# Laying the score matmuls right behind the weighted sums, in one step of a software pipeline

## The chip, the core and the metric

The kernel runs on one core of a Trainium2 chip. Time is device microseconds of one launch. The core has five engines that run side by side and meet in semaphores: PE (matmuls; the trace lists its weight loads apart as PEld), ACT, DVE, POOL and SP, which here only issues DMAs. Each engine takes its instructions strictly in the order in which the program lists them.

## What is computed

Attention with heads mixed before and after the softmax, then a layer of eight experts of which each token takes one, then a dense layer. The change lies in the attention:

```python
scores = scale * np.matmul(q, k.transpose(0, 1, 3, 2))      # batch 4, 12 heads, 448 x 448, head size 64
scores = np.einsum('bhij,hg->bgij', scores, w_pre)
attn = np.exp(scores - np.max(scores, axis=-1, keepdims=True))
attn = attn / (np.sum(attn, axis=-1, keepdims=True) + 1e-09)
attn = np.einsum('bhij,hg->bgij', attn, w_post)
x = np.matmul(attn, v)                                      # to [1792, 768]
x = _moe_ref(x, ...)                                        # top 1 of 8 experts, 768 -> 1024 -> 768
return _moe2_ref(x, ...)                                    # (h - tanh h) @ w_out, 768 -> 2048 -> 768
```

The weights of the last layer arrive as words of 64 bits; the kernel converts them on DVE and POOL while the attention runs ("conversion", 96 chunks, 72 of them inside the attention).

## The kernel before

**Tiles and steps.** The queries of each batch are cut into four tiles T of 120, 120, 120 and 88 rows, 16 tiles in all. A tile's scores (12 heads, in pairs p) are written to the buffer `s_sb`, of which there are two. A DMA, the relay `sr`, regroups them into blocks of ten queries by twelve heads, 120 partitions by 448 keys; a tile has 12 blocks or, where it is short, 9. There are 180 blocks, and the loop `for s in range(NBK + LAG + 6)` handles one a step:

- PE: P(s), the head mix before the softmax (L373); DVE: its row maximum `mx` (L377); ACT: the exponential p(s) with its sum (L380).
- DVE: `emit_W(s-1)`, which folds 1/sum into the mixing weights w (L387 to L390).
- PE: T(s-2), which turns and mixes in one go (four matmuls in the source, eight in the trace, L412); ACT: its copy into A (L417).

**Side work.** A table `side`, filled ahead of the loop by `at`, `at_s` and `at_e` from the position functions `posS2` and `posAV`, says in which step the rest stands: S2(T, p), the scores of two pairs for tile T, which the blocks need some ten steps later (L330; copies to `s_sb` at L337 and L334 on ACT, L335 on DVE); AV(T, p), weighted sums of the finished tile (L430, copy xT at L432 on ACT); `tr_q` and `tr_k`, the turned operands ptq and ptk; X, the turned outputs, with routing sums; R0 to R3 and M0 to M3, routing matmuls for the experts; and `conv_do`, one chunk of the conversion: three DVE operations (L117 to L119), three POOL operations, one store.

**A turned operand** passes four engines' queues: PE turns it into PSUM, ACT copies its high part (qh L310, kh L293), DVE writes the low part (ql L311, kl L294), and DVE does the latter in the next step, ahead of that step's row maximum:

```python
            for fn, a in turns:
                flush("e")
                late2.append(("e", fn(*a)()))     # turn, high part on ACT; low part put off
            if on:
                emit_TE(i)                        # ACT: A(s-2), behind that high part
```

**PSUM** has eight banks: P takes two in turn ("b"); T, R and M share two in turn ("c"); AV has one ("d"); ptq, ptk and X share one ("e"); S2 takes two of its own for its first pair of heads, and "d" and "e" for the second. So a turned operand can't start before the one ahead of it has left "e", and S2's second pair can't start before AV's result has left "d".

**Order within a step before:** P; row maximum; W; the first of S2 and AV that the step holds; the exponential; conversion; T; turned operands; A; what is left. S2 and AV stand as a rule in different steps. The 72 conversions stand in steps that hold S2 or AV, some of them two.

Of the kernel before, what the change touches and what calls it, by code (L numbers as in the profile page):

```python
# [30 lines left out]
def body(ctx: ExitStack, tc, q, k, v, w_pre, w_post, emb, tau, w1, w2, win, wout, out):  # L31
# [8 lines left out]
    NP = H // 2  # L40
# [89 lines left out]
    if True:  # L130
# [253 lines left out]
        def emit_W(i):  # L384
            n = 12 * blocks[i][2]
            p, mx = pj[i]
            dve.tensor_scalar_add(mx[:n, 2:3], mx[:n, 1:2], 1e-9)  # L387
            dve.reciprocal(mx[:n, 3:4], mx[:n, 2:3])
            w = a2.tile([120, 120], F32, tag="w", name=f"w{i}", bufs=3)
            dve.tensor_scalar_mul(w[:n, :], wpost[:n, :], mx[:n, 3:4])  # L390
            wj[i] = w
# [250 lines left out]
    with mctx:  # L642
# [334 lines left out]
        def posS(T, p):  # L977
            f, nb = (first[T - 1], ntile[T - 1]) if T else (-12, 12)
            return f - (5 if T > 1 else 3) + (p + 0.5) * nb / 6

        def posS2(T, p):
            return posS(T, p - p % 2 + 0.5)

        def posAV(T, p):
            f, nb = first[T + 1], ntile[T + 1]
            return f + LAG + 1 + p * nb / 6
# [48 lines left out]
        CA = CONV_A  # L1035
        kinds = lambda k: [x[0] for x in side.get(k, [])]
        routed = [k for k in side if emit_R in kinds(k)]
        free = [k for k in range(12, NBK - 11) if k not in routed]
        long_ = [k for k in free if emit_AV2 in kinds(k)]
        mid = [k for k in free if emit_S2 in kinds(k) and emit_AV2 not in kinds(k)]  # L1040
        alone = [k for k in long_ if not {emit_X, tr_q, tr_k} & set(kinds(k))]
        more = CA - len(long_) - len(mid)
        steps = sorted(long_ + mid + [alone[i * len(alone) // more] for i in range(more)])
        for j, st in enumerate(steps):
            ld = max(st - 4, steps[j - 4] + 1 if j >= 4 else 0)
            assert ld < st
# [22 lines left out]
        def relay_to(i):  # L1069
            while nxt[0] <= min(i, NBK - 1) and blocks[nxt[0]][0] in sdone:  # L1070
                emit_relay(nxt[0])
                nxt[0] += 1
# [4 lines left out]
        def flush(tag=None):  # L1077
            keep = []
            while late:
                x = late.pop(0)  # L1080
                if tag in (None, x[0]):
                    y = x[1]()
                    if x[0] == "e" and callable(y):
                        late2.append((x[0], y))
                else:
                    keep.append(x)
            late.extend(keep)
            if tag:
                flush2(tag)
# [9 lines left out]
        def run_fill(fn, a):  # L1099
            tag = "d" if fn is emit_AV2 else "e"  # L1100
            if fn is emit_S2:
                flush("d")
                flush("e")
            elif fn is not emit_S:
                flush(tag)
            e = fn(*a)
            if fn in (emit_S, emit_S2):
                e()
                if a[1] + (fn is emit_S2) == NP - 1:
                    sdone.add(a[0])  # L1110
            else:
                late.append((tag, e))
# [36 lines left out]
        for s in range(NBK + LAG + 6):  # L1149
            todo = side.get(s, [])  # L1150
            fill = [x for x in todo if x[0] in PEF]
            for fn, a in todo:
                if fn in (load_q, load_k, load_v, conv_load, zero_fill):
                    fn(*a)
            flush()
            relay_to(s + NSR - 1)
            ex = emit_P(s) if s < NBK else lambda: None
            if 0 <= s - 1 < NBK:
                emit_W(s - 1)
            for fn, a in todo:  # L1160
                if fn is emit_R and a[1] in (0, 1, 3):
                    fn(*a)
            i = s - LAG
            on = 0 <= i < NBK
            fill.sort(key=lambda x: x[0] not in (emit_S, emit_S2, emit_AV2))
            if fill and fill[0][0] in (emit_S, emit_S2, emit_AV2):
                run_fill(*fill.pop(0))
            ex()
            for fn, a in todo:
                if fn is conv_do:  # L1170
                    fn(*a)
            if on:
                emit_T(i)
                T_mm(i, 0, NJ)
                flush("d")
            turns = [x for x in fill if x[0] in (tr_q, tr_k)] if on else []
            for fn, a in turns:
                flush("e")
                late2.append(("e", fn(*a)()))
            if on:  # L1180
                emit_TE(i)
            for x in fill:
                if x not in turns:
                    run_fill(*x)
            for fn, a in todo:
                if fn in (to_experts, first_gather) or fn is emit_R and a[1] in (2, 4, 5, 6):
                    fn(*a)
            for fn, a in todo:
                if fn is do1:
                    fn(*a)  # L1190
# [55 lines left out]
        for n, e in enumerate(items):  # L1246
# [39 lines left out]
            todo = []  # L1286
            if not last:
                nw1, nx = [], xtile(f"i{n + 1}")
                todo = [lambda c=c: do1(n + 1, c, nw1) for c in range(KD)]
                todo += [lambda j=j, t=t, hf=hf: xsplit(nx, t, j, hf, f"i{n + 1}") for j, t in enumerate(nxg) for hf in range(2)]  # L1290
            for ci, col in enumerate(cols):
                y = mq[0].tile([128, DM], F32, tag="y", name=f"y{nm}_{ci}", bufs=2)
                for nh in range(2):
# [13 lines left out]
                    todo = todo[k_:]  # L1307
# [324 lines left out]
```

## Time and profile before

| what | value |
| --- | --- |
| median of 3 runs | 1296.83 us (1296.11 to 1299.66) |
| the profiled execution | 1295.99 us, of which 1294.1 us are the span from first to last instruction |
| PE busy | 1283.5 us (99%) |
| DVE, ACT, POOL busy | 1003.8, 747.7, 489.4 us (78, 58, 38%) |
| chain that ended last | PE 94%, DVE 2%, DMA 2%, ACT 1% |
| granted TensorE clock | 1.000 of full speed |

The times of the prediction are made against the profiled execution, 0.84 us below the median. The end of a matmul is modelled in the trace, so the sum of PE's busy time hides short waits; starts are what to read. A step is the time from one P to the next.

### The profile page before, as it was taken

The numbers are of one execution on the slowest core, as the hardware profiler recorded it, in microseconds if no ns is written. First come the engines' busy times: TensorE is split into PE (matmuls) and PEld (weight loads), VectorE is DVE, ScalarE is ACT, GpSimd is POOL, SyncE is SP. The second block draws the span as 40 slices with busy tenths as digits, with TensorE's granted clock in tenths as the row PEclk, the third lists the DMA queues.
The fourth block names the chain that finished last, engine by engine and source line by source line (L and its number), as shares of the span: only waits on it lengthen the run. The fifth ranks groups of instructions, "written<-read, shape, count | busy, mean of one in ns | idle before, by whom it ended". The sixth has DMA issues, their size and how long they took to land.

```text
span 1294.1 us, 24851 instructions
## 1 busy us (share of the span) xinstructions
PE 1283.5 (99%) x9072; PEld 1125.4 (87%) x9072; DVE 1003.8 (78%) x2168; ACT 747.7 (58%) x1513; POOL 489.4 (38%) x497
## 2 busy tenths in 40 slices
PE   9999999999999999999999999999999999999998
PEld 6777777777777778999999999999999999999997
DVE  5877877787878677788787676788888887888886
ACT  6767666666766665555544545765444556444432
POOL 1334423351344126333223222454644544444431
PEclk9999999999999999999999999999999999999999
DMA  7887665666557458778988876321211123111102
GB/s 172 268 267 214 199 204 152 200 202 192 160 168 223 147 157 301 262 264 250 268 245 259 265 241 210 105 86 49 86 58 65 49 99 122 50 50 49 50 25 88
DMA packets 153077, 210.95 MB, mean 163 GB/s; under 512 B 57686, under 2 KB 113158, under 8 KB 152950
## 3 DMA queue, kind: packets, MB, share of 16 engines
q1 hardware_dynamic: 149680, 195.37, 49.1%
q0 software_dynamic: 2480, 12.19, 2.7%
q8 instruction: 74, 1.21, 0.4%
q10 hardware_dynamic: 790, 1.74, 0.4%
q14 instruction: 53, 0.43, 0.1%
HBM read 135.71 MB, written 35.01 MB: 132 GB/s over the span
## 4 chain that ended last, share of the span: by engine, by line
PE 94%; DVE 2%; DMA 2%; ACT 1%; issue 0%; POOL 0%; SPq 0%; DVEq 0%; POOLq 0%
PE T L412 12%; PE P L373 10%; PE AV L430 6%; PE o L1454 6%; PE o L1452 6%; PE o L1453 6%; PE h L1418 6%; PE h L1417 6%; PE h L1416 6%; PE S L330 5%; PE ypi L706 3%; PE ypi L707 3%; PE ypi L705 3%; PE hi L729 3%; PE hi L730 3%; PE hi L731 3%
## 5 line engine op out<-in xcount | busy, mean ns | idle before, releaser
L412 PEld LDWEIGHTS T<-w,p 120*112 120x112 f32 (+1 forms) x1440 | 166.1, 177 | 59.5 <-issue 46.0
L122 POOL TENSOR_TENSOR cm<-cm,ct 128x256 f32<-128x256 f32 x96 | 70.7, 736 | 313.5 <-DVE ct L119 291.6
L412 PE MATMUL T<-w,p 120*112 120x120 f32 (+1 forms) x1440 | 185.0, 272 | 0.2 <-ACT p L380 0.2
L1399 POOL TENSOR_TENSOR gl<-th,gh 128x512 fp32r<-128x512 f32 (+1 forms) x64 | 77.5, 1211 | 241.1 <-ACT gh L1398 180.4
L373 PE MATMUL P<-sr,wpre 120*120 120x448 f32 x360 | 166.3, 544 | 1.0 <-DMA sr<-ssb 1.0
L380 ACT ACTIVATE p<-P,mx 120x448 f32<-120x448 f32 x180 | 114.1, 634 | 89.9 <-DVE mx L387 76.2
L1420 ACT ACTIVATE u<-h 128x512 f32<-128x512 f32 (+1 forms) x64 | 35.0, 547 | 204.1 <-PE h L1418 204.1
L1452 PE MATMUL o<-woh,gh 128*128 128x384 f32 x448 | 151.4, 338 | 0.0
L1454 PE MATMUL o<-woh,gl 128*128 128x384 f32 x448 | 150.4, 336 | 0.0
L1453 PE MATMUL o<-wol,gh 128*128 128x384 f32 x448 | 150.1, 335 | 0.0
L1458 DVE TENSOR_TENSOR acc<-acc,o 128x384 f32<-128x384 f32 x196 | 106.5, 548 | 47.2 <-PE o L1454 47.2
L377 DVE TENSOR_REDUCE mx<-P 120x1 f32<-120x448 f32 x180 | 111.6, 620 | 28.9 <-PE P L373 26.7
L120 POOL TENSOR_TENSOR cm<-craw 128x256 f32<-128x256 f32 x96 | 66.9, 697 | 112.8 <-DMA craw<-in_moe_w_in 59.2
L417 ACT COPY A<-T 112x480 f32<-112x480 f32 x180 | 102.3, 568 | 9.7 <-PE T L412 9.7
L729 PE MATMUL hi<-xhi,w1h 128*128 128x256 f32 x336 | 95.3, 283 | 0.0
L730 PE MATMUL hi<-xli,w1h 128*128 128x256 f32 x336 | 95.2, 283 | 0.0
L731 PE MATMUL hi<-xhi,w1l 128*128 128x256 f32 x336 | 95.2, 283 | 0.0
L705 PE MATMUL ypi<-w2hi,hhi 128*128 128x384 f32 x272 | 93.9, 345 | 0.0
L430 PEld LDWEIGHTS AV<-A,v 112*64 112x64 f32 x1536 | 73.9, 137 | 21.8 <-issue 10.7
L706 PE MATMUL ypi<-w2li,hhi 128*128 128x384 f32 x272 | 91.2, 335 | 0.2 <-DVE w2li L673 0.2
L707 PE MATMUL ypi<-w2hi,hli 128*128 128x384 f32 x272 | 91.2, 335 | 0.0
L121 POOL TENSOR_SCALAR cm<-cm 128x256 f32<-128x256 f32 x96 | 85.9, 895 | 8.4
(299 smaller groups left out, 3436.3 us busy)
## 6 DMA issues: line engine op xcount, KB each, us to landing
sr<-ssb SPq DMA_DIRECT2D x176, 210.0 KB
r<-in_moe_w SPq DMA_DIRECT2D x72, 384.0 KB
r<-in_moe_w SPq DMA_DIRECT2D x52, 512.0 KB
craw<-in_moe_w_in SPq DMA_DIRECT2D x48, 256.0 KB
craw<-in_moe_w_out SPq DMA_DIRECT2D x48, 256.0 KB
wor<-wo_d SPq DMA_DIRECT2D x16, 768.0 KB
raw<-wi_d SPq DMA_DIRECT2D x15, 768.0 KB
wi_d<-cm SPq DMA_DIRECT2D x48, 128.0 KB
```

What stands on the lines that cost most here:

```text
L373: pe.matmul(pt[:n, :S], wpre[:n, :n], t[:n, :], start=True, stop=True)
L412: pe.matmul(pt[:CP, c * n:(c + 1) * n] if m == 10 else pv[:, c], p[:n, c * CP:(c + 1) * CP], w[:n, :] if m == 10 else wv, start=True, stop ...
L430: pe.matmul(pt[64 * hh:64 * hh + 64, x * 120:x * 120 + n], vt[b, p + x][:, hh, c, :], A[T][:, c, 2 * (p + x) + hh, :n], start=c == 0, stop ...
L705: pe.matmul(pt[:, :384], a, wh[:, n0:n0 + 384], start=f == 0, stop=False)
L706: pe.matmul(pt[:, :384], a, wl[:, n0:n0 + 384], start=False, stop=False)
L707: pe.matmul(pt[:, :384], l, wh[:, n0:n0 + 384], start=False, stop=f == KF - 1)
L729: pe.matmul(pt[:, :256], wh[:, sl], xh[:, c, :], start=c == 0, stop=False)
L730: pe.matmul(pt[:, :256], wh[:, sl], xl[:, c, :], start=False, stop=False)
L731: pe.matmul(pt[:, :256], wl[:, sl], xh[:, c, :], start=False, stop=c == KD - 1)
L1452: pe.matmul(pt[:, :384], gh[:, sl], wo[0][:, f, n0:n0 + 384], start=f == 0, stop=False)
L1453: pe.matmul(pt[:, :384], gh[:, sl], wo[1][:, f, n0:n0 + 384], start=False, stop=False)
L1454: pe.matmul(pt[:, :384], gl[:, sl], wo[0][:, f, n0:n0 + 384], start=False, stop=f == GF - 1)
```

## The change

Three things. `posS2` puts S2(T, p) into the steps of AV, two places on: pairs 0 and 2 into the steps of AV(T-3, 2) and AV(T-3, 4), pair 4 into that of AV(T-2, 0). Since `tr_q`, `load_q`, `tr_k` and `load_k` are placed relative to `posS2`, they move with it. In a step with both, AV now comes ahead of S2, and the exponential and the conversion stand between them; T follows S2. And the conversions are dealt out anew: one a step over the steps with S2, AV or X, with a second one only where chunks are left.

```diff
         def posS2(T, p):
-            return posS(T, p - p % 2 + 0.5)
+            p -= p % 2
+            if p == NP - 2 and T > 1:
+                return posAV(T - 2, 0)
+            return posAV(T - 3, p + 2) if T > 2 else posS(T, p + 0.5)
...
-        alone = [k for k in long_ if not {emit_X, tr_q, tr_k} & set(kinds(k))]
-        more = CA - len(long_) - len(mid)
-        steps = sorted(long_ + mid + [alone[i * len(alone) // more] for i in range(more)])
+        both = [k for k in long_ if emit_S2 in kinds(k)]
+        rest_ = [k for k in free if emit_X in kinds(k) and k not in long_ + mid]
+        room = sorted(long_ + mid + rest_)
+        more = max(0, CA - len(room))
+        room = sorted(room + [both[i * len(both) // more] for i in range(more)])
+        steps = [room[i * len(room) // CA] for i in range(CA)]
...
             fill.sort(key=lambda x: x[0] not in (emit_S, emit_S2, emit_AV2))
+            fill.sort(key=lambda x: x[0] is not emit_AV2)
+            if len(fill) > 1 and fill[0][0] is emit_AV2 and fill[1][0] is emit_S2:
+                run_fill(*fill.pop(0))
+                ex()
+                ex = lambda: None
+                for fn, a in todo:
+                    if fn is conv_do:
+                        fn(*a)
+                todo = [x for x in todo if x[0] is not conv_do]
             if fill and fill[0][0] in (emit_S, emit_S2, emit_AV2):
                 run_fill(*fill.pop(0))
             ex()
```

In the rows of the built program below, the first number in a name is the step of P, T, w and p (P19 is step 19) or the tile of the rest, the last one only tells buffers apart.

PE from step 19 before: AV and S2 in two steps, each followed by its T.

```order
L373 MATMUL P19_932<-sr19_692,wpre_133 120x448
L430 MATMUL AV0_2_941<-A0_434,v0_2_443 64x120 x8
L430 MATMUL AV0_2_941<-A0_434,v0_3_463 64x120 x8
L412 MATMUL T17_968<-w17_919,p17_868 112x120 x4
L303 MATMUL ptq3_0_974<-ident_68,natq3_778 128x88 x3
L373 MATMUL P20_985<-sr20_713,wpre_133 120x448
L412 MATMUL T18_996<-w18_939,p18_916 112x120 x4
L373 MATMUL P21_1012<-sr21_759,wpre_133 120x448
L330 MATMUL S3_0_1022<-kh0_0_189,qh3_0_978 88x448 x2
L330 MATMUL S3_0_1022<-kl0_0_190,qh3_0_978 88x448 x2
L330 MATMUL S3_0_1022<-kh0_0_189,ql3_0_979 88x448 x2
```

PE in step 19 of the change, from the second half of AV: S2 follows AV, and T17 follows S2.

```order
L430 MATMUL AV0_2_942<-A0_434,v0_3_463 64x120 x8
L330 MATMUL S3_0_971<-kh0_0_189,qh3_0_899 88x448 x2
L330 MATMUL S3_0_971<-kl0_0_190,qh3_0_899 88x448 x2
L330 MATMUL S3_0_971<-kh0_0_189,ql3_0_900 88x448 x2
L330 MATMUL S3_1_0_978<-kh0_1_221,qh3_0_899 88x448
L330 MATMUL S3_1_1_979<-kh0_1_221,qh3_0_899 88x448
L330 MATMUL S3_1_0_978<-kl0_1_222,qh3_0_899 88x448
L330 MATMUL S3_1_1_979<-kl0_1_222,qh3_0_899 88x448
L330 MATMUL S3_1_0_978<-kh0_1_221,ql3_0_900 88x448
L330 MATMUL S3_1_1_979<-kh0_1_221,ql3_0_900 88x448
L412 MATMUL T17_989<-w17_914,p17_884 112x120 x4
L373 MATMUL P20_998<-sr20_713,wpre_133 120x448
```

So one T, with the whole array, that stood between AV and S2 is gone from there. Forty steps of the change read like this (15, 19, 23, ... to 162).

PE some steps on, before: a turned operand shares its step with AV, or has a step with AV or S2 on one side at least.

```order
L412 MATMUL T20_1069<-w20_1019,p20_990 112x120 x4
L287 MATMUL ptk1_0_1074<-ident_68,natk1_0_856 128x112 x4
L373 MATMUL P23_1087<-sr23_838,wpre_133 120x448
L430 MATMUL AV0_4_1097<-A0_434,v0_4_491 64x120 x8
L430 MATMUL AV0_4_1097<-A0_434,v0_5_516 64x120 x8
L412 MATMUL T21_1124<-w21_1066,p21_1016 112x120 x4
L303 MATMUL ptq3_1_1130<-ident_68,natq3_778 128x88 x3
L373 MATMUL P24_1141<-sr24_908,wpre_133 120x448
L412 MATMUL T22_1152<-w22_1095,p22_1063 112x120 x4
L287 MATMUL ptk1_1_1157<-ident_68,natk1_1_859 128x112 x4
L373 MATMUL P25_1176<-sr25_910,wpre_133 120x448
```

The same place of the change, steps 20 to 22: three turned operands in three steps one after the other, with nothing between them but P and T.

```order
L412 MATMUL T18_1008<-w18_940,p18_911 112x120 x4
L287 MATMUL ptk1_0_1013<-ident_68,natk1_0_778 128x112 x4
L373 MATMUL P21_1024<-sr21_759,wpre_133 120x448
L412 MATMUL T19_1035<-w19_1005,p19_937 112x120 x4
L303 MATMUL ptq3_1_1040<-ident_68,natq3_711 128x88 x3
L373 MATMUL P22_1053<-sr22_786,wpre_133 120x448
L412 MATMUL T20_1064<-w20_1032,p20_1002 112x120 x4
L287 MATMUL ptk1_1_1069<-ident_68,natk1_1_781 128x112 x4
L373 MATMUL P23_1088<-sr23_860,wpre_133 120x448
```

Such threes stand in steps 20 to 22, 24 to 26, 28 to 30, 65 to 67, 69 to 71, 73 to 75, 110 to 112, 114 to 116 and 118 to 120 (in 26, 71 and 116 the third is an X).

ACT around the routing of tile 4, before. On PE, R0 stands in step 64, ahead of AV and T62.

```order
L380 ACTIVATE p62_2603,mx62_2601<-P62_2599,mx62_2601 120x448
L417 COPY A5_2509<-T60_2636 112x48x10
L380 ACTIVATE p63_2650,mx63_2648<-P63_2646,mx63_2648 120x448
L417 COPY A5_2509<-T61_2656 112x48x10
L380 ACTIVATE p64_2668,mx64_2666<-P64_2664,mx64_2666 120x448
L432 COPY xT4_2540<-AV4_2_2682 128x240
```

ACT at the same place of the change. On PE, R0 now stands in step 63, a step without AV, straight ahead of T61; the seven DVE operations that feed it stand in step 61.

```order
L380 ACTIVATE p61_2583,mx61_2581<-P61_2579,mx61_2581 120x448
L417 COPY A5_2498<-T59_2598 112x48x10
L380 ACTIVATE p62_2610,mx62_2608<-P62_2606,mx62_2608 120x448
L310 CAST qh7_0_2625<-ptq7_0_2621 128x3x88
L417 COPY A5_2498<-T60_2616 112x48x10
L380 ACTIVATE p63_2636,mx63_2634<-P63_2631,mx63_2634 120x448
L417 COPY A5_2498<-T61_2651 112x48x10
```

What moved: the copy of T60 into A now stands behind the high part of ptq7_0, in the step just ahead of R0. M0 likewise moved from step 68, with AV, to step 67, without; R1, M1, R2 and M2 (steps 108, 112, 153, 157) read the same way.

## Rows read from the trace of the kernel before

**Rows 1.** Busy time of each engine in two stretches; x is the count of instructions.
```profile
core 0: us, PE busy (x) PEld busy (x) DVE busy (x) ACT busy (x) POOL busy (x), PEclk, DMA share, GB/s
40.00:493.00 453.00, 453.00 (x3971) 338.99 (x3969) 348.53 (x1076) 307.83 (x735) 162.16 (x223) 1.00 0.65 199
```

**Rows 2.** Timeline of steps 60 to 63, PE alone: start, length, engine, line, operation.
```profile
173.12 0.92 PE L373 MATMUL P<-sr,wpre 120*120 120x448 f32 x2
...
175.76 1.07 PE L412 MATMUL T<-w,p 120*112 120x120 f32 x8
...
176.67 0.92 PE L373 MATMUL P<-sr,wpre 120*120 120x448 f32 x2
...
177.42 0.98 PE L412 MATMUL T<-w,p 120*112 120x120 f32 x8
...
178.24 0.92 PE L373 MATMUL P<-sr,wpre 120*120 120x448 f32 x2
...
179.09 0.46 PE L330 MATMUL S<-kh,qh 64*120 64x448 f32 x2
...
179.80 0.37 PE L330 MATMUL S<-kh,qh 64*120 64x448 f32 x2
...
180.21 0.36 PE L330 MATMUL S<-kh,ql 64*120 64x448 f32 x2
...
181.41 0.92 PE L373 MATMUL P<-sr,wpre 120*120 120x448 f32 x2
```

**Rows 3.** Same timeline, ACT in step 60; in brackets idle time and releaser.
```profile
173.59 0.47 ACT L468 COPY raw<-X 88x384 f32<-88x384 f32 x1
...
174.10 0.84 ACT L477 ACTIVATE xsq<-raw 88x768 bf16<-88x768 f32 x1
...
175.87 0.36 ACT L432 COPY xT<-AV 128x240 f32<-128x240 f32 x1 [0.23 <-PE AV L430]
```

**Rows 4.** Timeline of steps 33 to 35, the chain through two turned operands.
```profile
99.58 0.92 PE L373 MATMUL P<-sr,wpre 120*120 120x448 f32 x2
...
100.54 0.62 DVE L377 TENSOR_REDUCE mx<-P 120x1 f32<-120x448 f32 x1
...
101.46 0.66 DVE L390 TENSOR_SCALAR w<-wpost,mx 120x120 f32<-120x120 f32 x1
101.47 0.92 PE L373 MATMUL P<-sr,wpre 120*120 120x448 f32 x2
...
101.89 0.45 ACT L310 CAST qh<-ptq 128x360 fp32r<-128x360 f32 x1
...
102.22 0.58 ACT L417 COPY A<-T 112x480 f32<-112x480 f32 x1
...
102.37 0.53 DVE L311 TENSOR_TENSOR ql<-ptq,qh 128x360 fp32r<-128x360 f32 x1 [0.24 <-ACT qh L310]
102.82 0.62 DVE L377 TENSOR_REDUCE mx<-P 120x1 f32<-120x448 f32 x1
...
103.73 0.28 DVE L390 TENSOR_SCALAR w<-wpost,mx 120x120 f32<-120x120 f32 x1
...
104.15 0.52 ACT L293 CAST kh<-ptk 128x448 fp32r<-128x448 f32 x1
...
104.71 0.62 DVE L294 TENSOR_TENSOR kl<-ptk,kh 128x448 fp32r<-128x448 f32 x1 [0.70 <-ACT kh L293]
...
105.25 0.62 DVE L377 TENSOR_REDUCE mx<-P 120x1 f32<-120x448 f32 x1
...
105.39 0.18 PEld L330 LDWEIGHTS S<-kh,qh 64*120 64x120 f32 x1 [0.31 <-DVE kl L294]
```

**Rows 5.** Timeline of step 62, the first and the last of seven routing operations.
```profile
180.31 0.18 DVE L498 TENSOR_TENSOR lk<-lg 128x32 f32<-128x32 f32 x1
...
181.65 0.19 DVE L508 TENSOR_TENSOR oht<-ohk,tokf 128x32 f16<-128x32 f16 x1
```

**Rows 6.** Timeline of step 178: a weight load for T and what released it.
```profile
491.70 0.89 PEld L412 LDWEIGHTS T<-w,p 120*112 120x112 f32 x8 [0.70 <-DVE idr L549]
```

## The prediction

> **What bounds the kernel now.** I read the windows first. From 40 to 493 us, the attention's steps 10 to 178, PE is busy in all 453 us, DVE in 349, ACT in 308, POOL in 162 [rows 1]. PE sets the time here, and any other engine matters only where it makes PE wait. Since matmul ends are modelled, I then read starts in PE's timeline [rows 2]. A step with only P and T takes 178.24 - 176.67 = 1.57 us, one with S2 3.17, one with AV 3.55. P to T is 0.75, T's eight matmuls take 0.82, or 0.1025 each. The other steps of the stretch repeat these lengths; a turned query adds 0.32 (101.47 - 99.58 = 1.89 [rows 4]), and I put a turned key, four transposes for three, at 1.97. So the kernel before has hardly a wait on PE, and the sum has two sides: PE work that goes, and waits that come.
>
> **What the change removes.** S2 adds 1.60 to a step. Its six pairs of matmuls go at (180.21 - 179.80) / 2 = 0.205, so 1.23 is streaming and 0.37 is the way in and out. AV adds 1.98; its 32 matmuls run two abreast, 16 places at T's 0.1025, so 1.64 is streaming and 0.34 the way in and out [rows 2]. Four switches between full and split array thus cost 0.71, one 0.18. AV, S2, T in one step has three switches where two steps had four: 0.18 saved, in 40 steps, **-7.2**. The trace has no AV with S2 straight behind it. The bounds are a passage that costs nothing (0.36 saved each, -14.4 in all) and one that costs two switches (nothing saved); I take one switch, since all four that can be read cost about the same.
> The Trainium skill bears on this one price: TensorEngine Tiling (Array Packing), section Key Properties, says that a change of tiling mode, not merely of the tile, drains the engine. AV splits the array by columns and S2 by rows, so by that rule the passage is a drain too and the sum stays; if only leaving the full array counted, the sum would be 7.2 lower. That the switches cost time [rows 2] agrees with it; no row shows this passage.
> Some waits of the kernel before go too. In steps 35, 80 and 125 S2's second pair waited for a key's low part in bank "e" (a weight load idle for 0.31, released by kl [rows 4]), 0.28 a step; T just ahead of them was 0.1 to 0.2 late behind a w that took 0.66 beside POOL in place of 0.28 [rows 4]; six S2 straight behind a turned key lose 0.08 each. Together **-1.8**. AV in between covers all these.
>
> **What it adds: a lag of DVE.** The row maximum starts 0.96 after P [rows 4]. From one maximum on: exponential done and high part started at +1.35 (100.54 to 101.89), A's copy from +1.68 (102.22), 0.58 long, low part from +1.83 (query, 0.53 long) or +1.89 (key, 0.62), the next step's maximum at +2.28 (query) or +2.43 (key). But a step with a turned operand takes PE only 1.89 or 1.97. So each such step sets DVE back by 0.4 to 0.5, and the next bears it. Before, an AV or S2 took up the lag almost everywhere; now steps with nothing but turned operands follow each other.
> *Three turned operands in a row.* From the first P: bank "e" is free again at 0.96 + 1.89 + 0.62 + 0.06 = 3.53 (0.06 from kl's end to the weight load [rows 4]), and the second wants it at 1.97 + 1.57 = 3.54: no wait. The second's maximum starts at 0.96 + 2.43 = 3.39. A query frees the bank at 3.39 + 1.83 + 0.53 + 0.06 = 5.81, a key at 5.96; the third wants it at 1.97 + 1.89 + 1.57 = 5.43 or at 5.51. Waits of 0.38 (four places) and 0.45 (three: 24 to 26, 69 to 71, 114 to 116): **+2.9**.
> *S2's second pair behind AV's copy.* Normally this is hidden: AV ends 2.64 after P, xT starts 0.11 later and takes 0.36 [rows 2, 3], so bank "d" is free at 3.17, and the second pair wants it at 2.64 + 0.71 = 3.35. xT stands behind the exponential, done at 2.31, 0.44 to spare. Behind a query between two keys the spare is gone: the combined step starts at 5.81 + 0.40 = 6.21, its maximum at 3.39 + 2.28 + 2.43 = 8.10, the exponential ends at 9.45, "d" is free at 9.87 and wanted at 9.56. 0.31 in four steps, 0.1 in the three behind an X: **+1.5**.
> *R and M ahead of T.* T in step 178 was released by idr [rows 6], the reader of M3, which stands two places earlier in the use of the bank pair "c" (M3 and a T in step 177): the two banks go strictly in turn. So T behind an R or M takes the bank of the T just before and must wait for that one's copy A. Before, AV's 1.98 stood between. Now, from step 61: maximum 0.96, W done at 0.96 + 0.62 + 0.58 = 2.16 (0.58 from 103.44 to 104.01 [rows 4]), then seven routing operations of 1.53 in all [rows 5]; so the maximum of step 62 starts at 3.65, the exponential ends at 5.00, the turned query's high part goes first, A's copy runs from 5.33 to 5.91 and T61 starts at 5.97. It could have at 1.57 + 1.89 + 0.75 + 0.1 for R = 4.31. 1.66 in each of steps 63, 108 and 153: **+5.0**. M in steps 67 and 112 has two turned operands ahead: A's copy ends at 3.39 + 1.68 + 0.58 = 5.65, T starts at 5.71 and not 4.71; 1.0 twice, which takes in the wait for "e" there, and 0.8 as an estimate in step 157, with one turned operand: **+2.8**.
> *Two X and then both, on a short tile* (steps 48, 93, 138). The copy of the turned output and its square, 0.47 + 0.84 on ACT, stand ahead of the exponential; in step 60 the square ended 1.82 after P, and the exponential behind it before xT began at 2.75 [rows 3]. AV of a short tile ends some 0.4 sooner, and the conversion in the X step now delays the maximum. I take 0.3 each: **+0.9**.
> *w beside POOL.* A w of 0.66 ends at 2.54, while T wants it at 1.57 + 0.75 = 2.32 if the next step has neither AV nor S2. There are about 13 such pairs of steps; behind a single conversion POOL is done within the long step, so I count four at 0.25: **+1.0**, with nothing and 3.5 as bounds.
>
> **What costs nothing.** The 72 conversions are the same work. In a combined step they lie under 4.97 us of PE; in X steps they lie under the wait for the turned output's copy on ACT, which holds back DVE's next maximum anyway; without that cover three operations of some 1.2 us would come on top of DVE's queue once per X, where PE has about 0.3 of slack. SP: q and k loads move with the turned operands, each still four or five steps ahead; relays go out seven steps ahead, and stores that wait for POOL stand ahead of one or two of them. P was held by none of them in a way that shows, PE being busy throughout [rows 1]. For a tile behind a short one the last scores come one step later than before, and its first relay still has five steps.
>
> **Sum.** 1295.99 - 7.2 - 1.8 + 2.9 + 1.5 + 5.0 + 2.8 + 0.9 + 1.0 = 1301.1 on the profiled execution's scale; the median of the runs lies 0.84 above it, so **1301.9 us**.
>
> **The rivals.**
> *A, the forecast*: the saving is nearly taken twice over by the lag. For it: the loop of 2.28 and 2.43 against 1.89 and 1.97 is measured, and one wait of its kind can be read [rows 4]. Against it: seven places out of one observation. With each wait a third smaller or larger, 1297 to 1307. Chance 0.55.
> *B, faster*: the lag doesn't build up. All of +2.9, +1.5, +5.0 and +2.8 hang on DVE's maximum standing behind the low part or the routing operations; if those ended in time, 1301.9 - 12.2 = 1289.7. For it: DVE idles 104 us of the 453 [rows 1]. Against it: that idle time lies in long steps. It decides for faster when these four terms come to 3.2 or less in place of 12.2. Chance 0.16.
> *C*: the passage AV to S2 is free: 1301.9 - 7.2 = 1294.7, no change that counts. Nothing in the rows speaks for it but that both are half arrays. Chance 0.16.
> *D*: the passage costs two switches, or waits are half as large again: 1309. The second would need further chains that I have overlooked. Chance 0.13.
>
> **How the numbers follow.** The runs of the kernel before spread over 3.5 us, so 0.3%, 3.9 us, is about what can be told from no change: faster is below 1292.9, slower above 1300.7. A gives slower 0.35 and same 0.20; B faster 0.13, same 0.03; C same 0.12, faster 0.03, slower 0.01; D slower 0.13. So faster 0.16, same 0.35, slower 0.49. The likeliest case alone spans 1297 to 1307; 1290 to 1308 reaches into B and D and leaves out about half of each.
>
> **What would show it.** Right: combined steps of 4.97 where nothing precedes them; T61, T106 and T151 starting right after the copy A of the T before, in steps about 1.6 too long; the third turned operand released by DVE's ql or kl; S2 in steps 23 and 31 released by xT. Wrong: combined steps of 4.8 or 5.15 (the passage); no wait in steps 22, 26, 63, 67 (the lag); or P waiting for a relay, which would be a term that I left at nothing.

## The result

The changed kernel took 1305.33 us (median of 7 runs, 1302.82 to 1308.68) where the kernel before, run beside it, took 1297.24: ratio 1.0056, 95% interval 1.0040 to 1.0071. It is slower by more than the 0.3% that can be told, within the range forecast and 3.4 us above the forecast itself.

The profiled execution took 1305.96 us, its span 1303.9. The windows view of the changed kernel, from the start of step 10 to that of step 178; the same 168 steps took 450.85 us in the kernel before (39.96 to 490.81).

```profile
core 0: us, PE busy (x) PEld busy (x) DVE busy (x) ACT busy (x) POOL busy (x), PEclk, DMA share, GB/s
39.90:497.03 457.13, 449.24 (x3959) 336.85 (x3958) 341.63 (x1068) 312.64 (x730) 161.05 (x220) 1.00 0.65 195
```

In [rows 1] PE had no idle time at all; now it idles for 457.13 - 449.24 = 7.9 us, and the attention is 6.3 us longer. The waits can be read where the prediction put them. First, PE's timeline of step 60, which answers to [rows 2]:

```profile
172.67 0.92 PE L373 MATMUL P<-sr,wpre 120*120 120x448 f32 x2
173.51 1.86 PE L430 MATMUL AV<-A,v 112*64 112x120 f32 x32
175.30 0.47 PE L330 MATMUL S<-kh,qh 64*120 64x448 f32 x2
...
176.72 1.07 PE L412 MATMUL T<-w,p 120*112 120x120 f32 x8
177.63 0.92 PE L373 MATMUL P<-sr,wpre 120*120 120x448 f32 x2
```

The step takes 177.63 - 172.67 = 4.96, where P and T alone (1.57), AV (1.98) and S2 (1.60) add up to 5.15: 0.19 saved. The other combined steps of a full tile, where nothing waits in them, take 4.92 to 4.97.

Next the timeline of step 63, which holds R and starts at 181.04; PEld is the weight load, and what stands in brackets is idle time and releaser:

```profile
181.15 0.62 DVE L377 TENSOR_REDUCE mx<-P 120x1 f32<-120x448 f32 x1
...
182.75 0.58 ACT L417 COPY A<-T 112x480 f32<-112x480 f32 x1
...
183.37 0.89 PEld L412 LDWEIGHTS T<-w,p 120*112 120x112 f32 x8 [1.30 <-ACT A L417]
...
184.29 0.92 PE L373 MATMUL P<-sr,wpre 120*120 120x448 f32 x2
```

The maximum at 181.15 is that of step 62, whose P started at 179.20: 1.95 late behind the routing operations of [rows 5], not the usual 0.96. The copy A behind it ends at 183.33, and T61 starts then; the step takes 3.25 where P and T take 1.57. M in step 67 is the same picture:

```profile
194.22 0.58 ACT L417 COPY A<-T 112x480 f32<-112x480 f32 x1
...
194.85 1.07 PE L412 MATMUL T<-w,p 120*112 120x120 f32 x8 [0.67 <-ACT A L417]
```

Of turned operands, the X behind two keys (step 26) and S2's second pair (step 31), in the same timeline:

```profile
81.91 0.95 PE L464 MATMUL X<-ien,xT 128*120 128x136 f32 x6 [0.18 <-DVE kl L294]
...
97.07 0.35 ACT L432 COPY xT<-AV 128x240 f32<-128x240 f32 x1
97.47 0.18 PEld L330 LDWEIGHTS S<-kh,qh 64*120 64x120 f32 x2 [0.46 <-ACT xT L432]
```

Each is released by the instruction that the prediction named, the low part of the key and the copy xT. Steps 22 and 23 read otherwise:

```profile
68.91 0.61 POOL L120 TENSOR_TENSOR cm<-craw 128x256 f32<-128x256 f32 x1 [5.05 <-DMA craw<-in_moe_w_in]
68.93 0.67 DVE L390 TENSOR_SCALAR w<-wpost,mx 120x120 f32<-120x120 f32 x1
...
69.75 1.04 PE L412 MATMUL T<-w,p 120*112 120x120 f32 x8 [0.36 <-ACT qh L310]
```

T in step 22 starts 1.31 behind its P (68.44) and not 0.75. It reads w and p but not qh, so I put this down to its w, which began 0.02 behind a POOL operation and took 0.67 in place of 0.28. In r_in_av below, which has the same program up to there, that T starts together with qh, not behind it: w takes 0.28, step 22 loses 0.28, and in step 23 S2's second pair waits for xT, as forecast. Steps 22 and 23 together are as long in both kernels, 7.51 and 7.52.

**Every step against its parts.** I compared each step of the two profiles (from P to P) with the sum of its parts: P and T 1.57, AV 1.98 (1.55 on a short tile), S2 1.60, a turned query 0.31, a turned key 0.39, X 0.70. What a step takes beyond that is called its excess below. By kind, changed kernel less kernel before:

| term | forecast | measured |
| --- | --- | --- |
| switches, 40 combined steps | -7.2 | -7.7 |
| old waits gone | -1.8 | -2.3 |
| third turned operand in a row | +2.9 | +3.6 |
| S2's second pair behind xT | +1.5 | +1.0 |
| R ahead of T | +5.0 | +4.7 |
| M ahead of T | +2.8 | +2.7 |
| two X, then both, short tile | +0.9 | +0.9 |
| w late beside POOL; conversions | +1.0 | +3.3 |
| attention | +5.1 | +6.3 (sum of the rows: 6.2) |
| outside the attention | 0 | +3.6 in this profile |

**Outside the attention.** From step 178 to the end of the span the code is the same; it took 803.3 us before and 806.9 now. The timeline at the first gather of expert outputs, of the changed kernel and then of the kernel before:

```profile
805.42 1.74 POOL L845 DMA_INDIRECT yg<-y_d,sgn  x1 [20.54 <-DVE hli L759]
...
811.58 1.62 PE L691 MATMUL xty<-dg,yg 128*128 128x128 f32 x6 [2.09 <-DMA yg<-y_d,sgn]
```

```profile
798.73 1.06 POOL L845 DMA_INDIRECT yg<-y_d,sgn  x1 [19.97 <-DVE w2li L673]
...
803.81 0.91 PE L691 MATMUL xty<-dg,yg 128*128 128x128 f32 x6 [0.48 <-DMA yg<-y_d,sgn]
```

PE's first matmul on the data started 6.16 us after the gather did and not 5.08, PE had waited 2.09 and not 0.48, and in the stretch behind that wait the granted clock was 0.52 (its lower level, 1.2 GHz), as the windows view of the changed kernel has it:

```profile
811.50:815.00 3.50, 3.42 (x16) 3.45 (x16) 0.56 (x1) 0.48 (x1) 2.59 (x4) 0.52 0.98 342
```

Of the kernels below, all with the same code there, spaced and rm_conv have this drop of the clock in their profiles too and the others don't; from step 178 to the end they take 807 and 811 us, the others 803 to 807. So I don't count these 3.6 us to the change. The medians differ by 8.1, though, of which the attention of the profile explains 6.3; the rest stays open.

### The profile page after: what moved, and what is told of

It reads as the page before. It is cut to its first block, busy times and chain, and to the rows that moved or that the text cites. A ratio compares the mean times of both kernels' runs of the same rounds, so it can differ in the third digit from the quotient of the medians.

```text
span 1303.9 us, 24755 instructions
## 1 busy us (share of the span) xinstructions
PE 1283.5 (98%) x9072; PEld 1126.1 (86%) x9072; DVE 999.2 (77%) x2168; ACT 753.8 (58%) x1513; POOL 490.8 (38%) x497
## 4 chain that ended last, share of the span: by engine, by line
PE 89%; DVE 5%; ACT 2%; DMA 2%; issue 1%; POOL 1%; SPq 0%; POOLq 0%; ACTq 0%; DVEq 0%
PE T L412 10%; PE P L373 8%; PE o L1469 6%; PE o L1467 6%; PE o L1468 6%; PE h L1432 6%; PE h L1433 6%; PE h L1431 6%; PE AV L430 6%; PE S L330 5%; PE ypi L706 4%; PE ypi L705 4%; PE ypi L707 4%; PE hi L729 3%; PE hi L730 3%; PE hi L731 3%
```

## The experiments

All are compared by the time from step 10 to step 178 in their profile, read off PE's timeline, and by the median of the runs. Ratios are to the kernel before, run on the same chip (medians there 1296.8 to 1298.5).

| kernel | steps 10 to 178, us | median, us | ratio, 95% interval |
| --- | --- | --- | --- |
| before | 450.85 | 1297.24 | |
| changed | 457.13 | 1305.33 | 1.0056 (1.0040 to 1.0071) |
| r_in_av | 450.81 | 1297.58 | 1.0006 (0.9995 to 1.0018) |
| conv2_late | 459.01 | 1304.07 | 1.0051 (1.0033 to 1.0068) |
| old_order | 470.29 | 1317.51 | 1.0158 (1.0132 to 1.0184) |
| old_conv | 456.24 | 1303.10 | 1.0050 (1.0033 to 1.0066) |
| conv_plan | 455.63 | 1303.04 | 1.0039 (1.0021 to 1.0056) |
| spaced | 460.62 | 1309.44 | 1.0078 (1.0056 to 1.0099) |
| order_only | 449.93 | 1295.64 (one run) | |
| best3 | 456.89 | 1305.42 | 1.0048 (1.0031 to 1.0066) |
| rm_conv | 450.95 | 1298.26 | 1.0003 (0.9992 to 1.0015) |
| rm_conv_keys | 450.34 | 1297.32 | 0.9993 (0.9982 to 1.0005) |
| keys_spread | 457.37 | 1304.04 (one run) | |
| order_only_timed | 449.83 | 1297.71 | 0.9988 (0.9974 to 1.0002) |

### R and M (r_in_av)

```diff
-                        at(e + y, emit_R, gi, x)
+                        at(e + y + (gi < len(RG) - 2), emit_R, gi, x)
```

> Router matmuls R and M one step later, so that they fall into the steps that have AV and S2 (64 and 68 for the second block of columns, and so on): one constant changed. Theory (T behind R or M takes the bank of the T just ahead and must wait for its copy A, which comes late because the routing operations stand ahead of the next maximum on DVE; an AV in between hides it): steps 63, 108 and 153 fall from 3.24 us to about 1.6, steps 67, 112 and 157 lose 0.7 to 1.0 each, the steps that now hold R and M stay within 0.2 of 4.97; in all about 7 us less, a time near 1298 where the changed kernel took 1305. Rival (R and M cost their step that time wherever they stand, by their own matmuls and by DVE's routing operations): steps 64, 109 and 154 become about 6.6 us long, the time stays at 1305.

PE's timeline of r_in_av, steps 63 and 64:

```profile
181.52 0.94 PE L373 MATMUL P<-sr,wpre 120*120 120x448 f32 x2
182.30 0.98 PE L412 MATMUL T<-w,p 120*112 120x120 f32 x8
183.12 0.92 PE L373 MATMUL P<-sr,wpre 120*120 120x448 f32 x2
183.87 0.18 PE L514 MATMUL R<-ohk,tri 128*128 128x32 f16 x1
...
184.15 1.86 PE L430 MATMUL AV<-A,v 112*64 112x120 f32 x32
...
187.32 1.07 PE L412 MATMUL T<-w,p 120*112 120x120 f32 x8
188.23 0.92 PE L373 MATMUL P<-sr,wpre 120*120 120x448 f32 x2
```

Step 63 takes 1.60 where it took 3.25, and step 64, with R in it, 5.11 where it took 4.94. The attention is 6.3 us shorter, the kernel is level with the one before, and the same matmuls and the same routing operations are still done. But the edit moved more than R and M. The rule that deals out the conversions passes over steps that hold R or M; in r_in_av's trace steps 76, 121 and 138 hold one conversion in place of two, and steps 27, 72 and 117 two in place of one. So the 6.3 us have to be read by steps. The six steps that lost R or M are 7.1 us shorter, the six that took them in 1.4 longer: 5.7 for R and M alone. Steps 78, 79, 123, 124 and 140 lose another 2.5 us with the conversions, and 1.9 came elsewhere, nearly all in steps 28, 29, 73, 74, 118 and 119. It is the place of R and M ahead of a T that has no AV in between that cost these 5.7 us; the rival falls.

### The passage from AV to S2 (order_only, order_only_timed, old_order)

order_only is the kernel before with the last hunk of the change alone (the lines from `fill.sort(key=lambda x: x[0] is not emit_AV2)` to `todo = ...`).

> The kernel before with the last hunk of the change alone: in the six steps of it that have AV and S2 (35, 42, 80, 87, 125, 132) AV, S2, T in place of S2, T, AV; all positions as before. Theory (AV straight to S2 saves one switch): steps 42, 87 and 132 fall from 5.05 to 4.97 and the steps behind them lose the 0.10 that they had, 0.18 each; steps 35, 80 and 125 fall from 5.41 to 4.97, since AV covers the wait for bank e, and lose 0.10 in the next; about 2 us in all, 1294 on a profile of 1296. Rival (the passage is free): 0.36 each; rival (it costs two switches): steps 42, 87 and 132 with the next as long as before, 6.72 together.

The windows of steps 42 and 43 in order_only, and then in the kernel before:

```profile
124.10:129.06 4.96, 4.96 (x56) 3.76 (x55) 3.64 (x12) 3.63 (x8) 1.45 (x3) 1.00 0.85 263
129.06:130.63 1.57, 1.57 (x12) 1.18 (x11) 0.61 (x2) 0.57 (x1) 0.71 (x1) 1.00 0.66 238
```

```profile
124.48:129.54 5.06, 5.06 (x57) 3.72 (x55) 3.65 (x12) 3.62 (x8) 0.76 (x2) 1.00 0.85 263
129.54:131.21 1.67, 1.67 (x13) 1.28 (x11) 0.62 (x2) 0.36 (x1) 1.38 (x2) 1.00 0.47 161
```

6.53 in place of 6.73: 0.20, which is one switch, for the passage alone, with the same work in the same steps. A free passage would have given 0.36, a passage of two switches nothing. The attention is 0.9 us shorter and not 2: step 35 still takes 5.26, and steps 38, 83 and 128 lose 0.16 each. Timed:

> The kernel of order_only, timed: its attention was 0.9 us shorter than that of the kernel before in one profile (449.9 against 450.8 us from step 10 to step 178), and nothing else differs. Theory (a switch saved in six steps and the wait for bank e covered in three, with the waits of steps 38, 83 and 128 against it): 0.9993 of the kernel before, just what a measurement of this kernel can't tell from no change. Rival (the profile's 0.9 us were chance): 1.0000.

0.9988, with an interval that takes in 1. If it is faster than the kernel before, it is by less than can be told.

old_order keeps the positions of the change and drops that same hunk.

> The positions of the changed kernel, but inside a step the order of the kernel before: S2, exponential, conversions, T, AV. Theory (a passage from AV straight to S2 saves one of four switches of 0.18 us): combined steps of 5.15 us in place of 4.97, 40 times, +7.4; against that S2's wait for bank d goes (-1) and the score copy stands ahead of the conversions again (-2 to -3); T behind R or M waits as before; in all +3 to +5, a time near 1309. Rival (the 0.18 came from the positions, two fillings in one step between the same two P and T, and not from the order): combined steps stay at 4.97, and the time falls to about 1302.

The switch came back as expected: combined steps take 5.05, and the steps behind them 0.10 more, 40 times. But the attention is 13.2 us longer than the change's, and not 3 to 5: with S2 at the head of the step, waits that AV had covered come out. In step 19, which has an excess of 0.97, S2's score copies start 0.7 us behind S2, the one on DVE released by a relay, and AV waits for the last of them:

```profile
64.42 1.86 PE L430 MATMUL AV<-A,v 112*64 112x120 f32 x32 [1.01 <-ACT ssb L334]
```

Steps 37, 54 and 99 lose 0.6 more each; in 54 and 99 it is T that waits, for w. I had taken the order to be worth one switch; it is also cover for the score copies.

### Conversions (conv2_late, old_conv, conv_plan)

My first reading of the changed trace was that two conversions ahead of S2's copy are what delays the maxima. The timeline of the changed kernel, steps 137 to 140:

```profile
394.38 0.92 PE L373 MATMUL P<-sr,wpre 120*120 120x448 f32 x2
394.59 0.28 DVE L117 TENSOR_SCALAR ct<-craw 128x256 int32<-128x256 int32 x1
...
395.44 0.42 DVE L119 SCALAR_TENSOR_TENSOR ct<-craw,ct 128x256 int32<-128x256 int32 x1
395.87 0.61 DVE L377 TENSOR_REDUCE mx<-P 120x1 f32<-120x448 f32 x1
...
396.78 0.61 DVE L390 TENSOR_SCALAR w<-wpost,mx 120x120 f32<-120x120 f32 x1
...
397.32 0.28 DVE L117 TENSOR_SCALAR ct<-craw 128x256 int32<-128x256 int32 x1
...
399.78 0.72 DVE L119 SCALAR_TENSOR_TENSOR ct<-craw,ct 128x256 int32<-128x256 int32 x1
...
400.42 0.61 DVE L335 TENSOR_SCALAR ssb<-S 120x448 f32<-120x448 f32 x1
...
402.29 1.04 PE L412 MATMUL T<-w,p 120*112 120x120 f32 x8 [0.59 <-DVE w L390]
```

The P at 394.38 is that of step 138. Its maximum comes 1.49 later, behind the conversion of the X step (395.44); w takes 0.61; two conversions fill DVE to 400.50; the score copy comes at 400.42, and T in step 140 waits for its w. Two kernels tried this reading.

```diff
-                for fn, a in todo:
-                    if fn is conv_do:
-                        fn(*a)
-                todo = [x for x in todo if x[0] is not conv_do]
+                cv_ = [x for x in todo if x[0] is conv_do]
+                for fn, a in cv_[:1]:
+                    fn(*a)
+                todo = [x for x in todo if x not in cv_[:1]]
```

> In the seven combined steps that have two conversions only the first one is left ahead of S2, the second goes behind it. Theory (with both ahead, S2's score copy on DVE comes behind 3 us of conversions, after the next P, and the next maxima, W and T are late by it): the excess of 0.2 to 0.8 us in steps 54, 78, 79, 99, 123, 124 and 140, together some 3.2 us, falls below 1 us, the time to about 1302. Rival (DVE has as much to do either way, and the copy of w only swaps places with the conversion): the same steps stay as long within 0.1 each, time 1305; the excess would then be from the conversions themselves.

The attention grew by 1.9: steps 54 and 99 went from 0.2 to 0.81 of excess, 78 and 123 from 0.48 to 0.60. The second conversion, behind the copy, stands just ahead of the next maximum. old_conv takes the rule of the kernel before for the steps of the conversions.

> The positions and the order of the changed kernel, but the 72 conversions spread as before: two in nearly every combined step, none in the steps with an X. Theory (two conversions ahead of the score copy delay DVE by some 1 us, which shows on PE in the next steps where neither an AV nor an S2 follows): 23 more such steps, where the seven of the changed kernel cost about 0.45 each; at 0.2 to 0.45 each +5 to +10, less the 0.9 of the three places with two X ahead of a combined step, whose conversions go; a time of 1309 to 1314. Rival (conversions cost nothing as long as DVE idles a fifth of the time): 1305, or 1304 by the steps with X.

The theory missed: the attention is 0.9 us shorter. The total is near the rival's, 1304 by the steps with X, but conversions aren't free by steps: 2.2 us went in steps 78, 79, 123, 124 and 140, 0.7 in 48, 93 and 138, and 2.1 came in steps such as 25, 29, 50, 74 and 119. With two conversions in step 121 but none in the X step 122, the excess of 123 and 124 fell from 0.87 to 0.05. I took that to mean the conversion in the X step and not the pair, and conv_plan deals them out by it. That was half of it. r_in_av has one conversion in step 121 and one in the X step 122, and there, too, the excess of 123 and 124 is 0.05:

```profile
350.88 0.61 DVE L377 TENSOR_REDUCE mx<-P 120x1 f32<-120x448 f32 x1
...
351.78 0.53 DVE L390 TENSOR_SCALAR w<-wpost,mx 120x120 f32<-120x120 f32 x1
352.42 1.02 PE L412 MATMUL T<-w,p 120*112 120x120 f32 x8
```

The maximum of step 123 comes 1.10 behind its P (349.78), where it came 1.84 behind in the changed kernel, and T in step 124 starts 0.76 behind its P (351.66), although w took 0.53. So the wait of these two steps needs both, the pair and then a conversion in the X step behind it; with either alone it is gone. In step 140 the pair in 138 costs 0.34 alone (old_conv), with the X step's conversion 0.82, and that conversion with a single one in 138 costs 0.04 (r_in_av).

```diff
-        rest_ = [k for k in free if emit_X in kinds(k) and k not in long_ + mid]
-        room = sorted(long_ + mid + rest_)
...
+        room = long_ + mid
+        for more in ([k for k in long_ if k not in short and turns_(k) < 2], pair, [k - 1 for k in pair], ...):
+            more = [k for k in more if room.count(k) < 2]
+            n = min(len(more), CA - len(room))
+            room += [more[i * len(more) // n] for i in range(n)]
```

Here `short` are the combined steps of a short tile, `turns_` counts the turned operands in the three steps behind, and `pair` are the second X steps of a pair that isn't just ahead of a short tile's step.

> The changed kernel with only the places of the 72 conversions changed: one in each combined step of a short tile, none in a single X step or in an X step just ahead of a short tile's combined step, two in the long combined steps without several turned operands behind them, the rest in pairs of X steps. Theory (a conversion in an X step is not covered: it delays the maximum behind it, and two in the shorter combined step of a short tile do too; in a long combined step two cost nothing): the excess of steps 78, 79, 123, 124, 140 (2.6 us in the changed kernel), of 54, 95 and 99 (0.6) and of 48, 93 and 138 (0.9) goes, about 4 us less, 1301. Rival (two conversions ahead of the score copy cost their 0.4 wherever they are, as I first read the trace): 16 long steps with two in place of 4 give back 3 to 5 us, 1304 to 1307.

The same steps 137 to 140 in conv_plan:

```profile
392.36 0.92 PE L373 MATMUL P<-sr,wpre 120*120 120x448 f32 x2
...
393.52 0.61 DVE L377 TENSOR_REDUCE mx<-P 120x1 f32<-120x448 f32 x1
...
394.43 0.28 DVE L390 TENSOR_SCALAR w<-wpost,mx 120x120 f32<-120x120 f32 x1
...
395.41 0.42 DVE L119 SCALAR_TENSOR_TENSOR ct<-craw,ct 128x256 int32<-128x256 int32 x1
...
396.16 0.62 DVE L335 TENSOR_SCALAR ssb<-S 120x448 f32<-120x448 f32 x1 [0.33 <-PE S L330]
...
399.26 1.02 PE L412 MATMUL T<-w,p 120*112 120x120 f32 x8
```

The maximum comes 1.16 behind P and not 1.49, w takes 0.28, the copy comes ahead of the next P, and no T waits. Steps 138 to 141 lose 1.03 us, 76 to 79 and 121 to 124 0.8 each, 48 to 59 0.44: the places named went as expected, and with pairs in the long steps. The attention lost 1.5 and not 4, mostly because the list put two conversions into steps 162 and 166 (steps 164 and 168 then wait 0.35 and 1.13; in rm_conv, with one each, they don't) and step 111 now waits 0.34.

### Turned operands (spaced, keys_spread)

```diff
-                e = posS2(4 * b - 1, p) + 1
+                e = int(posS2(4 * b - 1, p)) + p % 2
...
-                at_e(e, tr_k, b, p)
+                at_s(e, tr_k, b, p)
...
-            at_e(posS2(T, 0) - 2, tr_q, T, 0)
-            at_e(posS2(T, 2) - 2, tr_q, T, 1)
+            at_e(int(posS2(T, 0)) - (1 if T > 2 else 2), tr_q, T, 0)
+            at_e(int(posS2(T, 2)) - (1 if T > 2 else 2), tr_q, T, 1)
```

> The changed kernel with only the turned operands laid otherwise: keys in the combined step itself, behind its T, and in the step after it, queries in the last step ahead of a combined step, so that no three steps with turned operands follow one another (an X takes some of the places that they left). R and M stay where they are. Theory (each step with a turned operand sets DVE back by 0.4 to 0.5 us, which shows at the third in a row and in the bank that S2's second pair waits for): the excess of steps 22 to 31, 70 to 76 and 115 to 121, some 2 us in each of the three blocks, falls to under 0.5 in each, M in 67 and 112 from 1.14 to about 0.75; 4 to 5.5 us less, 1300 to 1301. Rival (a turned operand costs its wait wherever it stands, since DVE's work per step is the same): the same 5.5 us turn up in other steps, 1305.

Slower than theory and rival, by 3.5 us in the attention. The waits moved: 0.76 to 0.78 in front of each query that closes a stretch with two keys (steps 22, 30, 75, 120), 0.43 and 0.13 in the X pairs, and 1.28 and 1.52 in M's steps 67 and 112, where a query now follows in the step. Here, too, more moved than the turned operands: an X now stands in steps 25, 70 and 115, with a conversion, and no longer in 32, 77 and 122. keys_spread thins the keys out instead.

```diff
-                e = posS2(4 * b - 1, p) + 1
+                e = int((posS2(4 * b - 1, 0), posS2(4 * b - 1, 2), posS2(4 * b - 1, 2) + 1, posS2(4 * b - 1, 4), posS2(4 * b, 0), posS2(4 * b, 2))[p]) + 1
```

> The changed kernel with the keys of rm_conv_keys alone; conversions by the changed kernel's own rule, R and M where they are. Theory (number of turned operands between two combined steps): the excess of steps 22, 23, 29, 30, 31, 67, 74 to 76, 112 and 119 to 121 goes, 4 to 5 us in the attention, which is to end near 488.5 to 493 on the scale on which the changed kernel's step 178 starts at 497.0. Rival: 497 as before.

The rival has it: 457.37. The two kernels take 56.34 and 56.21 us from step 19 to step 39, and differ by 0.3 in each of the blocks behind. Where a third turned operand is gone, the X (which moved there from step 32, with its conversion) or the bare step in its place waits: step 22 0.22, step 30 0.43, step 34 0.34, steps 37 and 38 0.23 together. So in these places the third short step waits whatever it holds.

### Together (best3, rm_conv, rm_conv_keys)

best3 is r_in_av, spaced and conv_plan in one.

> Three repairs together on the changed kernel: R and M in the combined steps, turned operands spaced, the conversions by the list of conv_plan. Theory (the added waits are those named, and they add up): 1297.6 with R and M moved, less 4 to 5 for the turned operands, less about 3.5 for the conversions: 1289 to 1291, below both kernels by 0.4% or more. Rival (what DVE must do per step comes back as a wait elsewhere when one is taken away): not below 1295.

The rival: with the turned operands of spaced, all that R and M gave is lost again (step 64, for one, now holds R and a key and has an excess of 0.39, where other combined steps save 0.19). rm_conv leaves spaced out and gives steps 162 and 166 one conversion each.

> The changed kernel with R and M in the combined steps and the conversions as in conv_plan, but one in place of two in steps 162 and 166. Theory (the two sorts of wait are apart from one another): what is left of conversions' waits in r_in_av, 3.5 us in steps 27 to 29, 48, 54, 73, 74, 93, 95, 99, 118, 138 and 144, falls below 0.5, the time from 1297.6 to about 1294.5, just below the kernel before. Rival (a wait that is taken away comes back elsewhere, as it did in spaced): 1297 to 1298.

Again the rival: 450.95, nothing below r_in_av. The excess in steps 54, 73, 95, 99, 138 and 144 did go, but 0.41 came in step 65, 0.80 in step 110 and 0.47 in step 25. In step 110 it begins with the score copies, by the timeline of rm_conv:

```profile
314.90 0.91 ACT L337 ACTIVATE ssb<-S 88x896 f32<-88x896 f32 x1 [2.30 <-DMA sr<-ssb]
314.91 0.62 DVE L335 TENSOR_SCALAR ssb<-S 88x448 f32<-88x448 f32 x1 [2.96 <-DMA sr<-ssb]
...
315.88 1.07 PE L412 MATMUL T<-w,p 120*112 120x120 f32 x8 [0.54 <-DVE carry L525]
```

Both wait for a relay that has not yet read the score buffer they write to. Behind the one on DVE stands `carry`, which reads the result of the R in step 109, and T waits for it. In step 65 T is released by `carry` as well (0.16).

> As rm_conv, and the six keys of a block turned at most two between two combined steps that also turn a query, over five such intervals in place of three (steps 20, 24, 25, 28, 32, 36 in place of 20, 22, 24, 25, 28, 30). Theory (the lag of DVE is made up only under a combined step, so what counts is the number of turned operands between two of them, not their distance): the excess of steps 22, 23, 29, 30, 31 and of those that answer to them in the other two blocks goes, about 1.4 us a block; that of step 26 (0.5) stays, since two keys and an X still follow one another there; 1290 to 1291. Rival (a turned operand brings its wait wherever it stands): as rm_conv, 1294.5.

450.34, 0.9993 with an interval that takes in 1: level with rm_conv, as the rival said, and far from the 1290 to 1291 of the theory. No version came out below the kernel before by more than can be told.

## Why the prediction was right

**The sum.** It forecast +5.1 us in the attention, and the profile shows +6.3; forecast 1301.9, measured 1305.33. The range, 1290 to 1308, was wide enough for a faster kernel, too, so it is the table that speaks for the working: seven of its eight terms in the attention came within 0.7 of their forecast. One sum in the working is off: 2.16 + 1.53 is 3.69, not 3.65, for the maximum of step 62. Measured, it started 3.52 behind the P of step 61 (181.15 - 177.63).

**The switches.** One passage, one switch: order_only shows 0.20 for it alone, and old_order gives it back. The Trainium skill, TensorEngine Tiling (Array Packing), Key Properties, says that a change of tiling mode drains the engine; by that rule the passage from AV's columns to S2's rows costs a switch too. These runs agree: 0.20 us went with one passage fewer, where a free one would have given 0.36.

**R and M.** The largest wait (7.8 forecast, 7.4 measured) came where and as it was derived: DVE's routing operations, then the maximum, the copy A, and T behind it in the other bank of "c". r_in_av shows it by taking it away: 5.7 us in these steps, where the steps that R and M moved into are 0.2 to 0.3 longer. Rival B, that the lag doesn't build up, falls.

**Turned operands.** Waits of 0.38 in steps 30, 75 and 120, as forecast; 0.51 for 0.45 at the X. Steps 22 and 23, where I had put 0.38 and 0.31, lost 0.61 and nothing; that the sum is near is luck in this profile, since the 0.61 (in the third row of the table) came by a late w, as read above. r_in_av, without it, shows 0.28 and 0.33 where I had put them. What I had not seen is that the third step waits in keys_spread without a turned operand too. Moving them cost 3.5 us of the attention in spaced, gave nothing in keys_spread, and gave 0.6 in rm_conv_keys against rm_conv.

**The term that was mis-sized.** "w beside POOL" at +1.0, with the sentence that the 72 conversions cost nothing, measured +3.3 (the upper bound was 3.5). What failed is that sentence: a conversion in an X step lies under the wait for ACT's copy only where no pair of conversions stands in the combined step next to it. In the changed kernel the pair in step 121 makes the maximum of step 122 late by 0.3, the conversion there makes that of step 123 late by 0.9, and T in step 124 waits for a w that takes 0.60. With either the pair or the X step's conversion alone, these waits are gone. conv_plan took away 3.7 us of this term and of the two X's by other places for the conversions alone, though it lost more than half of that elsewhere.

**Outside the attention** I forecast nothing, and the profile shows 3.6 us that other kernels with the same code there mostly don't; that they aren't the change's is argued from their spread and not shown by a run of its own. The same holds for the rest of the 8.1 us between the medians.

## What to carry to other kernels

Where one engine is busy throughout, laying two of its long pieces together saves a switch of 0.2 us each time and at the same time takes the cover from every step that is left short: ask first which chain of the other engines (here DVE, ACT, DVE of 2.3 to 2.4 us) is then longer than a step. A wait derived from a place in a bank's rotation can be cured by moving the one instruction, as R and M were; a wait that comes from the total length of such a chain moved on in the two kernels that moved its parts alone or nearly so (spaced, keys_spread). Where a rule deals out work by what else a step holds, moving one entry moves others: compare the two programs by steps before you put a difference down to the entry. And of work "under cover" ask how much slack the next two steps have, not only this one.

## What was not expected of the hardware

The clock at 811.50 to 815.00 us, 0.52 granted, followed a wait of PE of 2.09 us for a gather, and the same drop followed waits of 1.94 and 1.80 there in spaced and rm_conv; in the kernel before, a wait of 0.48 at the same place was followed by no drop. The first matmul on the first gather's data started 5.08 us after the gather in one execution and 6.16 in the other.

A w beside POOL seems to wait for POOL's operation to end. From step 10 to step 178, 42 w's of the kernel before and 39 of the changed one took more than 0.30 us; all of the former and 37 of the latter ended 0.06 to 0.11 us behind the end of a POOL operation that overlapped them.
